# Packed attention before two feed-forward blocks: values loaded in long runs, 32x32 products, exponentials turned by VectorE, no zero-padded scores

## The chip, the cores and the metric

The kernel runs on one core of a Trainium2 chip. A run is one launch of the whole program; its time is the device time in microseconds (us). Before the change three runs gave 1664.1, 1665.73 and 1666.33 us, median 1665.73.

## What is computed

The inputs are q, k and v of shape (8 batches, 8 heads, 576 rows, 64) and p of shape (8, 8, 32, 64). For each batch and head the 32 packed queries p attend to k and v, and q then attends to the 32 results. The output, 4608 tokens of 512 features, goes through two feed-forward blocks:

```python
def sm_attn(qq, kk, vv):
    s = scale * np.matmul(qq, kk.transpose(0, 1, 3, 2))
    s = s - np.max(s, axis=-1, keepdims=True)
    a = np.exp(s)
    a = a / (np.sum(a, axis=-1, keepdims=True) + 1e-09)
    return np.matmul(a, vv)
p_packed = sm_attn(p, k, v)
out = sm_attn(q, p_packed, p_packed)
...
xn = x / rms * rms_g
g = xn @ w_gate
silu = g * (1.0 / (1.0 + np.exp(-g)))
x = silu * (xn @ w_val) @ w_out
h = x @ w_in
out = (h * np.cos(h)) @ w_out
```

Sums and products are in float32; the weights come as float64 and are narrowed to float32 on the chip.

## The kernel before, in words

The program has three parts. The **key stage** computes p_packed for all batches and heads, the middle part runs the first feed-forward block beside the second attention of the batches 1 to 7, and the last part runs the second block. The change touches the key stage alone.

The key stage is the loop `for i in range(NG + 2)` with NG = 16. A step i works on one group of four heads, whose four times 32 packed queries fill 128 partitions. Its work is spread over three steps of the loop, in an order written out by hand (`tc.manual_schedule()`), so that each engine runs its instructions in the order of the code:

- `load_k(i + 4)` and `load_v(i + 2)` issue the loads of k, p and v on the DMA queue of SyncE (SP). One k tile holds 18 rows of 64 values per partition, one run of 4608 bytes. One v tile is laid out as 4 heads x 6 rows per partition on 96 partitions, shifted by 16 (`V_P`), with zeros around them; it is loaded by three DMAs of 32 partitions each, in runs of 6 rows, 1536 bytes. There are three v tiles (`v_t`), used in turn.
- `u_prep` and `u_kt` turn p (`pt`) and k (`kp`, nine transposes) on TensorE. VectorE copies p back (`pT`), ScalarE copies k back (`kT`).
- `u_s1` computes the scores `s`: eight products, 64 rows of k deep. For i < S_PAD = 11 the stationary operand is padded with zeros from 32 to 128 columns, and the four heads add into the same 128 partitions. For i >= 11 each head writes its own 32 partitions. VectorE takes the maximum.
- `u_e` computes the exponentials `e` on ScalarE, into one buffer with 16 zero columns on either side (`e_pad`).
- `u_et`, one step later, turns e by six TensorE transposes of 96 (padded to 128) columns, which ScalarE copies back (`eT`).
- `u_pp`, in the same step, multiplies by v: 24 products, 128 rows deep, 32 columns out, 64 wide, into `pp`. VectorE then scales `pp` by the reciprocal of the sum into `cd` (two buffers), which SP stores to DRAM as `c`.
- `u_fin`, another step later, turns `cd` (`tp`), stores it as `q` through `tf`, and keeps it for the weights (`ppT`).

Beside this the loop carries two kinds of background work. From i = 1 to 16 it loads 19 pieces of the first block's weights (`w_load`, tile `wo`, 512 KB each) and narrows each in the next step: ScalarE takes the upper half (`w_prep(n, 0)`), VectorE runs four passes over it (`w_prep(n, 1)`, lines 143 to 153, called by `w_late`), and every second result is stored as `wy`. From i = 5 on it also carries the second attention of batch 0, as a generator that is advanced by three steps in each pass (`bg0_step`), with instructions on TensorE (`qtp`, `sp`, `xp`), ScalarE (`sq`) and VectorE (`at`, `ssq`). Three products of packed values and weights (`unit`, tile `mps`) lie in the passes 6, 10 and 14.

The order inside one pass decides what waits:

```python
        if 0 < i <= NG: u_et(i - 1)
        if i < NG: u_s1(i)
        ...
        bg0_step(i, 1)
        if 0 < i <= NG: u_pp(i - 1)
        ...
        bg0_step(i, 0 if i == U_ATT else 2)
        ...
        load_v(i + 2)
```

The stores that a pass collects are issued at the top of the next pass (`store(0)`), after the loads of weights and of k and ahead of `load_v`. PSUM buffers of the tag `kp` (four) are shared by `pt`, `kp`, `et`, `tp` and `pp` in turn.

When the loop has ended, TensorE begins the first block with the products `gv` (line 158), which need the second attention of batch 0 (`apt`). On ScalarE's queue the split of `apt` stands behind the last `tf`.

Of the kernel before, what the change touches and what calls it, by code (L numbers as in the profile page):

```python
# [9 lines left out]
F32 = mybir.dt.float32  # L10
F32R = mybir.dt.float32r
I32 = mybir.dt.int32
AF = mybir.ActivationFunctionType
# [7 lines left out]
def kernel(  # L21
# [14 lines left out]
    nc = tc.nc  # L36
    B, H, S, D = q.shape
    NP = p.shape[2]
# [3 lines left out]
    CP = 96  # L42
    NC_ = S // CP
    HALF = S // 2
    CH = NC_ // 2
# [4 lines left out]
    NG = 2 * B  # L50
# [9 lines left out]
    BG_B, KP_B = 2, 4  # L60
    WO_U = 4
    REST = S - 512
    V_P = 16
    R_LOAD, R_SPLIT, S_AT = (1, 2), (4, 5), (20, 21, 24 + 1, 24 + 2)
    W_FROM, W_TO = 1, 16
    W_ORD = (0, 1, 2, 3, 16, 4, 5, 6, 17, 7, 8, 18, 9, 10, 11, 19, 12, 13, 14)
    W_KV = 16
    ATT_U, U_ATT = 28, 5
    S_PAD = 11
    U_S = {6: 0, 10: 1, 14: 2}  # L70
    U_AT = {3: (0, 3), 8: (0, 4), 14: (0, 5), 16: (1, 0), 18: (1, 1), 20: (1, 2), 22: (1, 3), 26: (1, 4), 30: (1, 5)}
    U_J = (12, 15, 18, 21, 26, 30)
# [1 line left out]
    B0_W = (15, 16, 17, 18, 19, -4, 20, 21, -5, 22, 23, -6, 0, -7, 0, -8, 0, -9, 0, -10, 0, -11)  # L74
    B0_L, B0_LEAD = {15: (0,), 16: (1, 2), 17: (3,)}, 4
    W_LOAD, W_SPLIT = (4, 6, 14, 16), (9, 11, 17, 19)
    W2_I0, W2_POOL = 28, False
    T_END, F3_B, OWN = 2, 3, 16
    LAG, LAG_B = 3, 4
# [12 lines left out]
    ident = const.tile([128, 128], F32, name="ident")  # L92
# [87 lines left out]
    u5 = ust.enter_context(tc.tile_pool(name="u5", bufs=4))  # L180
    u2 = ust.enter_context(tc.tile_pool(name="u2", bufs=2))
    u1 = ust.enter_context(tc.tile_pool(name="u1", bufs=1))
    ps_2 = pst.enter_context(tc.tile_pool(name="ps_2", bufs=KP_B, space=PSUM))
# [5 lines left out]
    pT = u1.tile([128, 4, 160], F32, name="pT")  # L189
# [141 lines left out]
                fs[word[0]](int(word[1]), int(word[2]))  # L331
            yield nxt[:1]

    v_t = [u2.tile([128, 4, NC_, D], F32, tag=f"vn{x}", name="vn", bufs=1) for x in range(3)]
    for x in range(2):
        nc.vector.memset(v_t[x], 0.0)
    e_pad = u2.tile([128, 2 * V_P + S], F32, tag="e", name="e", bufs=1)
    for x in (slice(0, V_P), slice(V_P + S, 2 * V_P + S)):
        nc.vector.memset(e_pad[:, x], 0.0)
    nat_k, nat_v = {}, {}  # L340
    st = {}

# [10 lines left out]
    def load_v(i):  # L353
        if i >= NG:
            return
        b, g = divmod(i, 2)
        vn = nat_v[i] = v_t[i % len(v_t)]
        vs = v[b, 4 * g:4 * g + 4].rearrange("h (p m c) d -> m p h c d", m=CH, c=NC_)
        for m in (0, 2, 1):
            nc.sync.dma_start(out=vn[V_P + m * 32:V_P + (m + 1) * 32], in_=vs[m])  # L360

    load_k(0)
    for i in range(2):
# [7 lines left out]
    def u_prep(i):  # L371
        pn, kn = nat_k.pop(i)
        z = st[i] = {}
        nc.gpsimd.tensor_copy(pn[:, 1], pn[:, 0])
        pt = ps_2.tile([128, 128], F32, tag="kp", name="pt")
        nc.tensor.transpose(pt, pn.rearrange("p a d -> p (a d)"), ident)
        nc.vector.tensor_copy(pT[:, :, :NP], pt.rearrange("p (h n) -> p h n", h=4))
        z["kT"], z["kn"] = u1.tile([128, 4, HALF], F32, tag="kT", name="kT"), kn

    def u_kt(i, ms):  # L380

        z = st[i]
        kT, kn = z["kT"], z["kn"]
        kv = kT.rearrange("q h (t m p) -> q h t m p", t=CH, m=CH)
        for m in ms:
            kp = ps_2.tile([128, CH * 128], F32, tag="kp", name="kp")
            for t in range(CH):
                r = 2 * (CH * m + t)
                nc.tensor.transpose(
                    kp[:, t * 128:(t + 1) * 128], kn[:, r:r + 2, :].rearrange("p c d -> p (c d)"), ident  # L390
                )
            nc.scalar.activation(
                out=kv[:, :, :, m, :], in_=kp.rearrange("q (t h p) -> q h t p", t=CH, h=4), func=AF.Copy
            )

    def u_s1(i):
# [4 lines left out]
        for h in range(4):  # L401
            for r, rows in enumerate((top, bot)):
                if i < S_PAD:
                    nc.tensor.matmul(
# [11 lines left out]
    def u_e(i):  # L416
        z = st[i]
        s1, mx = z["s1"], z["mx"]
        e = e_pad[:, V_P:V_P + S].rearrange("p (a s) -> p a s", a=2)
        nc.scalar.activation(  # L420
            out=e, in_=s1[:, :, :HALF], func=AF.Exp, scale=scale, bias=mx[:, 1:2], accum_out=mx[:, 2:3]
        )

    def u_et(i):
        z = st[i]
        eT = u2.tile([128, NC_, 128], F32, tag="eT", name="eT", bufs=1)
        for hf in range(2):
            et = ps_2.tile([128, CH, 128], F32, tag="kp", name="et")
            for c in range(CH):
                cc = hf * CH + c  # L430
                nc.tensor.transpose(et[:, c, :], e_pad[:, cc * CP:cc * CP + 128], ident)
            nc.scalar.activation(out=eT[:, hf * CH:(hf + 1) * CH], in_=et, func=AF.Copy)
        z["eT"], mx = eT, z["mx"]
        nc.vector.tensor_scalar(out=mx[:, 2:3], in0=mx[:, 2:3], scalar1=1e-9, scalar2=None, op0=ALU.add)
        nc.vector.reciprocal(out=mx[:, 3:4], in_=mx[:, 2:3])

    def u_pp(i):
        b, g = divmod(i, 2)
        z = st[i]
        eT, vn, mx = z["eT"], nat_v.pop(i), z["mx"]  # L440
        pp = ps_2.tile([128, D], F32, tag="kp", name="pp")
        for c in range(NC_):
            for h in range(4):
                r = slice(h * NP, (h + 1) * NP)
                nc.tensor.matmul(
                    pp[r], eT[:, c, r], vn[:, h, c % CH * 2 + c // CH, :], start=c == 0, stop=c == NC_ - 1
                )
        cd = u2.tile([128, 2, D], F32, tag="cd", name="cd", bufs=2)
        nc.vector.tensor_scalar(
            out=cd, in0=pp.unsqueeze(1).to_broadcast([128, 2, D]), scalar1=mx[:, 3:4], scalar2=None, op0=ALU.mult  # L450
        )
        stores.append((c_dram[b][:, g, :], cd[:, 0, :]))
        z["cd"] = cd

    def u_fin(i):
        z = st[i]
        b, g = divmod(i, 2)
        tp = ps_2.tile([128, 4, NP], F32, tag="kp", name="tp")
        nc.tensor.transpose(tp.rearrange("p h n -> p (h n)"), z["cd"].rearrange("p a d -> p (a d)"), ident)
        tf = u2.tile([128, 4, NP], F32, tag="tf", name="tf", bufs=3)  # L460
        nc.scalar.activation(out=tf, in_=tp, func=AF.Copy)
        stores.append((q_dram[b][:, 4 * g:4 * g + 4, :], tf))
        n, t = b % 4, ppT[b // 4]
        nc.vector.tensor_tensor(
            out=t[:, 4 * g:4 * g + 4, n * NP:(n + 1) * NP], in0=tp,
            in1=gT[:, 4 * g:4 * g + 4].unsqueeze(2).to_broadcast([128, 4, NP]), op=ALU.mult
        )
        st.pop(i)
# [4 lines left out]
    def w_load(n):  # L473
        if n >= W_KV:
            wo_load(n - W_KV)
            return
        wy_load(n)
# [57 lines left out]
    def b0_load(x):  # L535
        if x < len(B0_W) and B0_W[x]:
            n = B0_W[x]
            (wy_load if n >= 0 else wo_load)(abs(n))
# [63 lines left out]
    def w_due(i):  # L602
        a, b = (n_w * max(0, min(x, W_TO) - W_FROM) // (W_TO - W_FROM) for x in (i, i + 1))
        return [W_ORD[x] for x in range(a, b)]
# [10 lines left out]
    order.enter_context(tc.manual_schedule())  # L615
    u_prep(0)
    u_kt(0, range(CH))
    nc.gpsimd.memset(v_t[2], 0.0)
    w_q, wo_q = [], []
    w_late = lambda: None  # L620
    for i in range(NG + 2):
        due = list(w_due(i))
        for n in due:
            w_load(n)
        load_k(i + 4)
        for n in B0_L.get(i, ()):
            b0_load(n)
        if i == 1:
            load_q()
            load_q()  # L630
        store(0)
        if i == U_ATT:
            att_load(0)
            att_load_c(0)
        if 0 < i <= NG:
            u_et(i - 1)
        if i < NG:
            u_s1(i)
        if i + 1 < NG:
            u_prep(i + 1)  # L640
            u_kt(i + 1, [0, 1])
        if 1 < i:
            u_fin(i - 2)
        if i <= NG:
            w_late()
        if i < NG:
            u_e(i)
        if i + 1 < NG:
            u_kt(i + 1, [2])
        for n in w_q:  # L650
            w_prep(n, 0)
        for n in wo_q:
            wo_split(n - W_KV, 0)
        bg0_step(i, 1)
        if 0 < i <= NG:
            u_pp(i - 1)
        if i in U_S:
            unit(0, U_S[i])
        bg0_step(i, 0 if i == U_ATT else 2)
        w_last = w_late  # L660

        def w_late(ns=tuple(w_q), os=tuple(wo_q)):
            for n in ns:
                w_prep(n, 1)
            for n in os:
                wo_split(n - W_KV, 1)
        if i < NG:
            w_late()
            w_late = lambda: None
        wo_q = [n for n in w_q if n >= W_KV]  # L670
        w_q = due
        load_v(i + 2)
# [187 lines left out]
    for i in range(len(seq) + LAG):  # L860
        b, f, hf = seq[min(i, len(seq) - 1)]
        j = i - b * B1
        if i < len(seq):
# [11 lines left out]
            t = gv_block(b, hf, f)  # L875
# [137 lines left out]
    for i in range(len(seq) + LAG_B):  # L1013
        if i < len(seq):
            n, f = seq[i]
# [16 lines left out]
        if LAG_B <= i < len(seq) + LAG_B - T_END:  # L1032
            n, f = seq[i - LAG_B]
# [33 lines left out]
```

## Time and profile before

| | us |
|---|---|
| median of three runs (1664.1 to 1666.33) | 1665.73 |
| the profiled execution | 1664.63 |
| its span | 1662.8 |
| its key stage, from the start of the span to the first `gv` product | 155.6 |
| TensorE (PE) busy, whole span | 1607.7 (97%) |
| VectorE (DVE) busy, whole span | 1006.9 (61%) |
| ScalarE (ACT) busy, whole span | 809.6 (49%) |

The span is the profiled time from the first to the last instruction of the core; 1.8 us of the execution's own time lie around it. [...] A TensorE product of float32 operands shows as two records, so 24 products are 48 records.

### The profile page before, as it was taken

How to read it: one execution, taken by the hardware profiler on the slowest of the kernel's cores; microseconds unless marked ns; L12 is line 12 of the kernel's file. 1: busy time of each engine (PE TensorE's matmuls, PEld its weight loads, DVE VectorE, ACT ScalarE, POOL GpSimd, SP SyncE). 2: the span in 40 equal slices, each digit the busy share in tenths (PEclk: the TensorE clock that was granted, in tenths of full speed). 3: DMA queues.
4: the chain of work that ended last, by engine and by line, in shares of the span. 5: the costliest groups of instructions: out<-in, count | busy, mean ns of one | idle time of the engine just before them, and what ended most of it. 6: DMA issues, size and time to landing. Idle time of an engine off the chain costs nothing.

```text
span 1662.8 us, 25654 instructions
## 1 busy us (share of the span) xinstructions
PE 1607.7 (97%) x9920; PEld 1308.2 (79%) x9920; DVE 1006.9 (61%) x1890; ACT 809.6 (49%) x1519; POOL 74.9 (5%) x74
## 2 busy tenths in 40 slices
PE   7767989999999999999999999999999999999998
PEld 5545768787888888888988888888888888888887
DVE  3567985666666656564426665656565656565554
ACT  3455554444454444443425555545454545454443
POOL 1000540000000000000210000000000000000000
PEclk9787999999999999999999999999999999999999
DMA  9996754454645453533372110101010101000001
GB/s 235 266 268 198 227 165 153 155 189 145 198 140 185 147 196 131 169 125 110 112 257 77 38 38 1 51 1 51 1 51 0 51 1 51 1 10 16 1 26 26
DMA packets 103577, 177.31 MB, mean 107 GB/s; under 512 B 39456, under 2 KB 55840, under 8 KB 103456
## 3 DMA queue, kind: packets, MB, share of 16 engines
q1 hardware_dynamic: 103456, 175.68, 34.9%
q8 instruction: 78, 1.28, 0.3%
q14 instruction: 43, 0.35, 0.1%
HBM read 134.22 MB, written 41.42 MB: 106 GB/s over the span
## 4 chain that ended last, share of the span: by engine, by line
PE 89%; DVE 4%; DMA 3%; ACT 1%; issue 1%; POOL 0%; SPq 0%; DVEq 0%; ACTq 0%; POOLq 0%
PE hp L159 8%; PE hp L160 8%; PE hp L158 8%; PE ops L160 8%; PE ops L159 8%; PE ops L158 8%; PE gv L158 6%; PE acc L158 6%; PE gv L159 6%; PE acc L160 6%; PE gv L160 6%; PE acc L159 6%; PE mps L565 3%; DMA c<-cd 2%; PE qtp L229 1%
## 5 line engine op out<-in xcount | busy, mean ns | idle before, releaser
L158 PE MATMUL gv<-apt,wmhl 128*128 128x288 f32 x768 | 234.0, 305 | 2.0 <-ACT apt L106 0.9
L159 PE MATMUL gv<-apt,wmhl 128*128 128x288 f32 x768 | 227.8, 297 | 0.4 <-DVE apt L107 0.4
L160 PE MATMUL gv<-apt,wmhl 128*128 128x288 f32 x768 | 226.8, 295 | 0.0
L159 PE MATMUL hp<-xhl,wmhl 128*128 128x512 f32 x576 | 224.1, 389 | 0.0
L160 PE MATMUL hp<-xhl,wmhl 128*128 128x512 f32 x576 | 224.1, 389 | 0.0
L158 PE MATMUL ops<-w2hl,ghl 128*128 128x512 f32 x576 | 224.1, 389 | 0.0
L159 PE MATMUL ops<-w2hl,ghl 128*128 128x512 f32 x576 | 224.1, 389 | 0.0
L158 PE MATMUL hp<-xhl,wmhl 128*128 128x512 f32 x576 | 223.9, 389 | 0.0
L160 PE MATMUL ops<-w2hl,ghl 128*128 128x512 f32 x576 | 222.3, 389 | 0.0
L966 ACT ACTIVATE r<-r 128x512 f32<-128x512 f32 x144 | 91.0, 632 | 250.0 <-DVE r L965 250.0
L974 DVE TENSOR_TENSOR r<-r,hp 128x512 f32<-128x512 f32 x144 | 98.9, 687 | 164.7 <-ACT r L967 164.7
L758 ACT ACTIVATE shl<-silu 128x288 fp32r<-128x288 f32 x192 | 85.4, 445 | 201.6 <-DVE silu L751 201.6
L158 PEld LDWEIGHTS gv<-apt,wmhl 128*128 128x128 f32 x768 | 145.0, 189 | 49.0 <-issue 15.3
L158 PE MATMUL acc<-shl,wohl 128*128 128x512 f32 x432 | 175.4, 406 | 1.1 <-ACT wohl L528 0.9
L160 PE MATMUL acc<-shl,wohl 128*128 128x512 f32 x432 | 170.4, 394 | 2.8 <-POOL wohl L531 2.8
L159 PE MATMUL acc<-shl,wohl 128*128 128x512 f32 x432 | 169.6, 393 | 0.0
L961 ACT ACTIVATE kk<-hp,magic 128x512 f32<-128x512 f32 x144 | 99.1, 688 | 117.4 <-PE hp L160 117.2
L751 DVE TENSOR_TENSOR silu<-silu,gv 128x288 f32<-128x288 f32 x192 | 86.4, 450 | 106.8 <-PE gv L160 81.9
L159 PEld LDWEIGHTS gv<-apt,wmhl 128*128 128x128 f32 x768 | 145.0, 189 | 5.9 <-DVE apt L107 0.6
L160 PEld LDWEIGHTS gv<-apt,wmhl 128*128 128x128 f32 x768 | 144.9, 189 | 0.0
L962 DVE TENSOR_SCALAR kk<-kk 128x512 f32<-128x512 f32 x144 | 61.4, 426 | 116.2 <-ACT kk L961 116.1
L159 PEld LDWEIGHTS ops<-w2hl,ghl 128*128 128x128 f32 x576 | 108.2, 188 | 22.6
(122 smaller groups left out, 2624.6 us busy)
## 6 DMA issues: line engine op xcount, KB each, us to landing
wy<-wy SPq DMA_DIRECT2D x96, 512.0 KB, 4.6
kn<-in_k_dram SPq DMA_DIRECT2D x16, 576.0 KB, 7.9
vn<-in_v_dram SPq DMA_DIRECT2D x48, 192.0 KB, 6.7
qnat<-in_q_dram SPq DMA_DIRECT2D x32, 288.0 KB, 4.1
x_dram<-x SPq DMA_DIRECT2D x18, 512.0 KB, 3.0
x1raw<-x_dram SPq DMA_DIRECT2D x18, 512.0 KB, 3.9
raw<-in_moe_w_in_dram SPq DMA_DIRECT2D x16, 512.0 KB, 4.3
raw<-in_moe_w_out_dram SPq DMA_DIRECT2D x16, 512.0 KB, 4.3
```

The costliest lines, as they stand in the source:

```text
L158: nc.tensor.matmul(ps, lhi, rhi, start=first, stop=False)
L159: nc.tensor.matmul(ps, lhi, rlo, start=False, stop=False)
L160: nc.tensor.matmul(ps, llo, rhi, start=False, stop=last)
L229: nc.tensor.transpose(tp[:, c * CP:(c + 1) * CP], qv[:, i, 2 * c:2 * c + 2, :].rearrange("p c d -> p (c d)"), ident[:CP, :CP],)
L565: nc.tensor.matmul(ps[kt][h * NP:(h + 1) * NP], ppT[b // 4][rows, 4 * kt + h, n:n + NP], w_y[2 * u + kt][rows, j], start=True, stop=True,)
L751: nc.vector.tensor_tensor(out=t, in0=t, in1=pss[1], op=ALU.mult)
L758: nc.scalar.activation(out=sh[:, 0, cols], in_=t, func=AF.Copy)
L961: nc.scalar.activation(out=kk, in_=hp, func=AF.Identity, scale=1.0 / TWO_PI, bias=magic[:, 0:1])
L962: nc.vector.tensor_scalar(out=kk, in0=kk, scalar1=-MAGIC, scalar2=None, op0=ALU.add)
L966: nc.scalar.activation(out=r, in_=r, func=AF.Abs)
L974: nc.vector.tensor_tensor(out=r, in0=r, in1=hp, op=ALU.mult)
```

## The change

Six edits, all in the key stage:

1. One v tile is now loaded like k, by one DMA on 128 partitions in runs of 18 rows (4608 bytes), into four buffers instead of three; the zero fills are gone.
2. The keys are written to `kT` in the order that fits this layout.
3. The exponentials are turned by VectorE, as 32x32 blocks in one instruction of 576 columns; the six TensorE transposes and the two ScalarE copies of each group are gone.
4. The product with v runs as 72 products of 32 rows and 32 columns instead of 24 of 128 rows.
5. The scaling of `pp` into `cd` is a function of its own (`u_cd`), called behind the narrowing at the end of a pass, and `cd` has four buffers instead of two (`tf` four instead of three). `pT` is copied back by ScalarE instead of VectorE.
6. S_PAD is 0: no scores are padded.

```diff
-    S_PAD = 11
+    S_PAD = 0
...
-    v_t = [u2.tile([128, 4, NC_, D], F32, tag=f"vn{x}", name="vn", bufs=1) for x in range(3)]
-    for x in range(2):
-        nc.vector.memset(v_t[x], 0.0)
-    e_pad = u2.tile([128, 2 * V_P + S], F32, tag="e", name="e", bufs=1)
...
-        vn = nat_v[i] = v_t[i % len(v_t)]
-        vs = v[b, 4 * g:4 * g + 4].rearrange("h (p m c) d -> m p h c d", m=CH, c=NC_)
-        for m in (0, 2, 1):
-            nc.sync.dma_start(out=vn[V_P + m * 32:V_P + (m + 1) * 32], in_=vs[m])
+        vn = nat_v[i] = u5.tile([128, CH * NC_, D], F32, tag="vn", name="vn", bufs=VB)
+        nc.sync.dma_start(out=vn, in_=v[b, 4 * g:4 * g + 4].rearrange("h (p c) d -> (h p) c d", c=CH * NC_))
...
-        nc.vector.tensor_copy(pT[:, :, :NP], pt.rearrange("p (h n) -> p h n", h=4))
+        nc.scalar.activation(out=pT[:, :, :NP], in_=pt.rearrange("p (h n) -> p h n", h=4), func=AF.Copy)
...
-        kv = kT.rearrange("q h (t m p) -> q h t m p", t=CH, m=CH)
+        kv = kT.rearrange("q h (c p) -> q h c p", p=NP)
...
-        e = e_pad[:, V_P:V_P + S].rearrange("p (a s) -> p a s", a=2)
+        e = z["e"] = u2.tile([128, 2, HALF], F32, tag="e", name="e", bufs=1)
...
-        eT = u2.tile([128, NC_, 128], F32, tag="eT", name="eT", bufs=1)
-        for hf in range(2):
-            et = ps_2.tile([128, CH, 128], F32, tag="kp", name="et")
-            for c in range(CH):
-                cc = hf * CH + c
-                nc.tensor.transpose(et[:, c, :], e_pad[:, cc * CP:cc * CP + 128], ident)
-            nc.scalar.activation(out=eT[:, hf * CH:(hf + 1) * CH], in_=et, func=AF.Copy)
+        eT = u2.tile([128, 2, HALF // NP, NP], F32, tag="eT", name="eT", bufs=1)
+        nc.vector.transpose(eT.rearrange("p a c n -> p (a c n)"), z["e"].rearrange("p a s -> p (a s)"))
...
-        for c in range(NC_):
+        n_c = CH * NC_
+        for c in range(n_c):
             for h in range(4):
                 r = slice(h * NP, (h + 1) * NP)
                 nc.tensor.matmul(
-                    pp[r], eT[:, c, r], vn[:, h, c % CH * 2 + c // CH, :], start=c == 0, stop=c == NC_ - 1
+                    pp[r], eT[r, c % 2, c // 2], vn[r, c], start=c == 0, stop=c == n_c - 1
                 )
-        cd = u2.tile([128, 2, D], F32, tag="cd", name="cd", bufs=2)
+        z["pp"] = pp
+
+    def u_cd(i):
+        b, g = divmod(i, 2)
+        z = st[i]
+        pp, mx = z["pp"], z["mx"]
+        cd = u2.tile([128, 2, D], F32, tag="cd", name="cd", bufs=4)
...
         if i < NG:
             w_late()
             w_late = lambda: None
+        if 0 < i <= NG:
+            u_cd(i - 1)
```

What this does to the order of instructions is shown at three places. First TensorE, from the end of the pass that multiplies by the values to the next pass (`pp` is the product with v, `et` the turned exponentials, `s` the scores, `pt` and `kp` the turned p and k). Before:

```order
L389 MATMUL kp<-ident,kn 128x128 x3
L445 MATMUL pp<-vn,eT 32x64 x24
L431 MATMUL et<-ident,e 128x128 x6
L404 MATMUL s_578<-kT,pT 128x288 x8
L376 MATMUL pt<-ident,pn 128x128
```

With the change:

```order
L381 MATMUL kp<-ident,kn 128x128 x3
L432 MATMUL pp<-vn,eT 32x64 x72
L400 MATMUL s_811<-kT,pT 32x288 x8
L368 MATMUL pt<-ident,pn 128x128
L381 MATMUL kp<-ident,kn 128x128 x6
```

The six transposes are gone, the scores are 32 columns wide instead of 128, and there are three times as many products with v.

Second VectorE, one pass with one piece of weights (`mx` is the maximum and the sum, `cd` the scaled result, lines 143 to 153 the narrowing). Before:

```order
L434 TENSOR_SCALAR mx<-mx 128x1
L435 RECIPROCAL mx<-mx 128x1
L412 TENSOR_REDUCE mx<-s_675 128x1
L413 TENSOR_SCALAR mx<-mx 128x1
L377 COPY pT<-pt 128x4x32
L464 TENSOR_TENSOR ppT_175<-tp,gT 128x4x32
L449 TENSOR_SCALAR cd<-pp,mx 128x128
L143 TENSOR_SCALAR wy<-wy 128x512
L145 TENSOR_SCALAR wy<-wy 128x512
L149 SCALAR_TENSOR_TENSOR wy<-wo,wy 128x512
L153 SCALAR_TENSOR_TENSOR wy<-wo,wy 128x512
```

With the change:

```order
L419 STREAM_TRANSPOSE eT<-e 128x576
L421 TENSOR_SCALAR mx<-mx 128x1
L422 RECIPROCAL mx<-mx 128x1
L404 TENSOR_REDUCE mx<-s_675 128x1
L405 TENSOR_SCALAR mx<-mx 128x1
L457 TENSOR_TENSOR ppT_175<-tp,gT 128x4x32
L143 TENSOR_SCALAR wy<-wy 128x512
L145 TENSOR_SCALAR wy<-wy 128x512
L149 SCALAR_TENSOR_TENSOR wy<-wo,wy 128x512
L153 SCALAR_TENSOR_TENSOR wy<-wo,wy 128x512
L442 TENSOR_SCALAR cd<-pp,mx 128x128
```

The transpose stands at the head of the pass, the copy of `pT` has left this engine, and `cd` has moved from ahead of the narrowing to behind it.

Third the DMA queue of SP, the same pass (`q`, `c` and `wy` are stores, the others loads). Before:

```order
L350 DMA kn<-in_k_dram 128x1152
L578 DMA q_72<-tf 128x128
L578 DMA c_65<-cd 128x64
L578 DMA wy_80<-wy 128x1024
L360 DMA vn<-in_v_dram 32x4x384 x3
```

With the change:

```order
L344 DMA kn<-in_k_dram 128x1152
L571 DMA q_72<-tf 128x128
L571 DMA wy_80<-wy 128x1024
L571 DMA c_65<-cd 128x64
L352 DMA vn<-in_v_dram 128x1152
```

The store of `c` now stands behind that of `wy`, and the three loads of v have become one.

## Rows read from the trace of the kernel before

**Rows 1.** Page, the span in 40 slices of 41.6 us.
```profile
PE   7767989999999999999999999999999999999998
...
PEclk9787999999999999999999999999999999999999
DMA  9996754454645453533372110101010101000001
```

**Rows 2.** Key stage: stretch, us, busy PE PEld DVE ACT POOL, clock, DMA share, GB/s.
```profile
0.00:32.50 32.50, 25.39 (x284) 18.81 (x284) 11.55 (x31) 14.18 (x33) 4.35 (x20) 1.00 0.99 235
32.50:115.30 82.80, 59.22 (x746) 39.94 (x744) 49.39 (x122) 39.05 (x93) 2.20 (x9) 0.80 1.03 268
115.30:155.60 40.30, 26.79 (x417) 17.15 (x416) 27.88 (x70) 21.26 (x52) 1.64 (x2) 0.78 0.78 210
```

**Rows 3.** Chain that ended last, 0 to 160 us: start, us, what.
```profile
30.18 9.20 DMA c<-cd
...
95.96 7.29 DMA c<-cd
```

**Rows 4.** Waits, 0 to 160 us: total, times, longest, in us.
```profile
POOL pn L374 <- DMA pn<-in_p_dram: 82.5, 12, 12.4
...
DVE cd L449 <- DMA c<-cd: 21.5, 6, 8.2
```

**Rows 5.** Three short stretches, columns as in Rows 2.
```profile
25.00:30.00 5.00, 5.00 (x81) 3.90 (x81) 3.39 (x9) 2.93 (x9) 0.24 (x1) 1.00 1.09 213
105.00:107.50 2.50, 2.50 (x54) 1.88 (x52) 2.37 (x6) 0.91 (x3) 0.29 (x1) 0.50 1.05 386
97.50:100.00 2.50, 1.81 (x16) 0.18 (x12) 2.42 (x8) 0.66 (x2) 0.00 (x0) 1.00 1.03 334
```

**Rows 6.** DMA packets by size: 25 to 30 us, then 105 to 107.5 us.
```profile
DMA packets 719, 1.06 MB, mean 213 GB/s; under 512 B 64, under 2 KB 700, under 8 KB 719
...
DMA packets 544, 0.96 MB, mean 386 GB/s; under 512 B 236, under 2 KB 349, under 8 KB 544
```

**Rows 7.** Groups by line and form, 0 to 160 us: busy us, mean ns, idle before.
```profile
L432 ACT ACTIVATE eT<-et 128x384 f32<-128x384 f32 x32 | 14.6, 493 | 7.1 <-PE et L431 6.5
...
L377 DVE COPY pT<-pt 128x128 f32<-128x128 f32 x16 | 4.5, 281 | 0.0
...
L276 DVE STREAM_TRANSPOSE at<-s 128x576 f32<-128x576 f32 x2 | 1.5, 766 | 0.0
```

**Rows 8.** TensorE in order of time (start, us): clock 1.00, then 0.50 from 106.13 on.
```profile
25.41 0.88 PE L445 MATMUL pp<-vn,eT 128*32 128x64 f32 x48
...
26.22 0.87 PE L431 MATMUL et<-ident,e 128*128 128x128 f32 x6
27.02 2.21 PE L404 MATMUL s<-kT,pT 64*128 64x288 f32 x16
...
101.03 0.72 PE L408 MATMUL s<-kT,pT 64*32 64x288 f32 x16
...
106.13 1.51 PE L445 MATMUL pp<-vn,eT 128*32 128x64 f32 x48
...
113.86 1.54 PE L431 MATMUL et<-ident,e 128*128 128x128 f32 x6
115.33 1.14 PE L408 MATMUL s<-kT,pT 64*32 64x288 f32 x16
```

**Rows 9.** TensorE in order of time: the scores of four passes, and one `mps`.
```profile
85.69 2.21 PE L404 MATMUL s<-kT,pT 64*128 64x288 f32 x16
...
91.86 2.21 PE L404 MATMUL s<-kT,pT 64*128 64x288 f32 x16
...
126.05 1.21 PE L408 MATMUL s<-kT,pT 64*32 64x288 f32 x16
...
136.29 1.21 PE L408 MATMUL s<-kT,pT 64*32 64x288 f32 x16
...
140.87 1.09 PE L565 MATMUL mps<-wy,ppT 64*32 64x512 f32 x16
```

More of the change, by code (lines that the diff above doesn't have):

```diff
@@ L62 @@
     REST = S - 512
-    V_P = 16
     R_LOAD, R_SPLIT, S_AT = (1, 2), (4, 5), (20, 21, 24 + 1, 24 + 2)
@@ L76 @@
     W_LOAD, W_SPLIT = (4, 6, 14, 16), (9, 11, 17, 19)
+    VB = 4
     W2_I0, W2_POOL = 28, False
@@ L332, in attend @@
             yield nxt[:1]
-    v_t = [u2.tile([128, 4, NC_, D], F32, tag=f"vn{x}", name="vn", bufs=1) for x in range(3)]
-    for x in range(2):
-        nc.vector.memset(v_t[x], 0.0)
-    e_pad = u2.tile([128, 2 * V_P + S], F32, tag="e", name="e", bufs=1)
-    for x in (slice(0, V_P), slice(V_P + S, 2 * V_P + S)):
-        nc.vector.memset(e_pad[:, x], 0.0)
     nat_k, nat_v = {}, {}
@@ L392, in u_kt @@
             nc.scalar.activation(
-                out=kv[:, :, :, m, :], in_=kp.rearrange("q (t h p) -> q h t p", t=CH, h=4), func=AF.Copy
+                out=kv[:, :, CH * m:CH * (m + 1), :], in_=kp.rearrange("q (t h p) -> q h t p", t=CH, h=4), func=AF.Copy
             )
@@ L437, in u_pp @@
     def u_pp(i):
-        b, g = divmod(i, 2)
         z = st[i]
-        eT, vn, mx = z["eT"], nat_v.pop(i), z["mx"]
+        eT, vn = z["eT"], nat_v.pop(i)
         pp = ps_2.tile([128, D], F32, tag="kp", name="pp")
-        for c in range(NC_):
+        n_c = CH * NC_
+        for c in range(n_c):
             for h in range(4):
@@ L459, in u_fin @@
         nc.tensor.transpose(tp.rearrange("p h n -> p (h n)"), z["cd"].rearrange("p a d -> p (a d)"), ident)
-        tf = u2.tile([128, 4, NP], F32, tag="tf", name="tf", bufs=3)
+        tf = u2.tile([128, 4, NP], F32, tag="tf", name="tf", bufs=4)
         nc.scalar.activation(out=tf, in_=tp, func=AF.Copy)
@@ L617 @@
     u_kt(0, range(CH))
-    nc.gpsimd.memset(v_t[2], 0.0)
     w_q, wo_q = [], []
```

## The prediction

> **What bounds the kernel now.** I read the 40 slices first, then the busy times by stretch, the chain of waits, the list of waits, and last short stretches and single instructions in order of time.
>
> The slices [rows 1] show two kernels in one. From the fifth slice on TensorE is at 9 tenths in all slices but two early ones, and its clock is granted in full; nothing in the key stage's code can speed that part. The first four slices are the key stage: TensorE at 6 to 9 tenths, its clock at 7 to 9 tenths, and the DMA engines at 9. The change can gain or lose only there, in the 155.6 us before the first `gv` product, and what it gains there the end of the program keeps, since the rest runs on TensorE.
>
> In the key stage no engine is full [rows 2]: between 32.5 and 115.3 us TensorE is busy 59.2 of 82.8 us, VectorE 49.4, ScalarE 39.1. The DMA share is 0.99 and 1.03 up to 115.3 us, so all 16 engines have packets under way, yet they move only 235 and 268 GB/s. After 115.3 us the share falls to 0.78: there something else sets the pace.
>
> The chain of waits blames the stores of `c`: five pieces, the first 9.20 us and the last 7.29 us long [rows 3]. The wait behind them is VectorE's: `cd` has two buffers, and its writer stood 21.5 us in six waits for an older store to land [rows 4]. But the store is slow because it stands in a full queue, and the loads of p, issued well ahead, make POOL wait 82.5 us in twelve waits [rows 4]. So I read the first 115 us as bound by what the DMA engines deliver, with the wait for `c` as the place where it shows.
>
> What do they spend their time on? From 25 to 30 us the packets are nearly all v's: 700 − 64 = 636 of 719 lie between 512 B and 2 KB, which at v's 1536 bytes is 0.98 of 1.06 MB [rows 6], and the rate is 213 GB/s at a share of 1.09 [rows 5]. From 105 to 107.5 us 544 − 349 = 195 packets above 2 KB, the runs of k (4608 bytes) and of the weights, carry most of 0.96 MB, at 386 GB/s and a share of 1.05; the stretch from 97.5 us moves 334 GB/s [rows 5, 6]. The same engines, as busy, move 1.6 to 1.8 times as much when the runs are long and reach all partitions.
>
> **The change part by part.**
>
> *Loads of v.* 16 groups of 3 × 192 KB = 589,824 bytes. At 213 GB/s one takes 2.77 us of the DMA engines. In k's form I take 360 GB/s, the middle of 334 and 386: 1.64 us. Saved: 1.13 us a group. 14 groups are issued before 115.3 us, where the DMA engines are the bound: **−15.8 us**. Ends: at the 268 GB/s that the stretch has as a whole a group takes 2.20 us, and the gain is 8.0; at 386 it takes 1.53, and the gain is 17.4. If v's short runs also hold up the other transfers, and all that is moved from 32.5 to 115.3 us went at 360 GB/s, that stretch would take 82.8 × 268 / 360 = 61.6 us, 21.2 less. That is about as far as it could go: VectorE has 49.4 us of work there, and two passes that did not wait for a store stand 6.2 us apart [rows 9], against 82.8 / 8 = 10.4 on average.
>
> *The wait for `c`* (21.5 us) goes with four buffers. By itself I cost that at nothing, because the full DMA queue covers it: without it VectorE and TensorE would next wait for p and k, as POOL does now. It is what lets the −15.8 through; with two buffers the writer would still meet the queue. Behind the moved `cd` on VectorE stands the next pass's transpose; who waits for `cd` is `tp`, a whole pass later, and the store. SP holds that store ahead of the load of v, so v is issued later in the pass by up to the narrowing. With four v buffers and two passes of lead I cost that at nothing; the cover is the lead of about 16 us. The queue also drops two DMA issues a group.
>
> *TensorE*, per pass at full clock [rows 8]: the turned exponentials go (−0.87), the scores shrink from 2.21 to 0.72 us in eleven passes (−1.49), and the product with v grows from 48 to 144 records. No row shows products of 32 rows and 32 columns on the diagonal. The nearest is the present `pp`, also four products side by side, 0.88 us for 48 records: three times that is 2.64 (+1.76). Net −0.6 in eleven passes, +0.9 in five. At half clock (1.54, 1.14, 1.51) the last five gain 3.02 − 1.54 = +1.5. TensorE is free for 23.6 of 82.8 us and 13.5 of the last 40.3 [rows 2], and `cd` now comes behind 2.2 us of narrowing, so I cost this at nothing inside the loop. In the last pass nothing follows but `cd`, `tp` and `gv`: **+1.0 us** there, the middle of +0.9 and +1.5 less what the narrowing hides; ends 0 and 1.5.
>
> *ScalarE* loses 32 copies of 493 ns (15.8 us by the mean, 14.6 busy) and takes over 16 of 281 ns [rows 7]: 10 us less, hidden, as it is busy half the time.
>
> *VectorE* takes over a transpose of 128x576; the attention's own takes 766 ns [rows 7]. The copy of `pT` (281 ns) leaves. Net +0.49 us a pass. Up to 115.3 us the DMA engines cover that. In the last stretch VectorE has the most work (27.9 of 40.3 us) [rows 2] and the passes follow each other at 10.2 us [rows 9], VectorE's queue waiting in turn for ScalarE and TensorE: five passes, **+2.4 us**; ends 0 and 5 × 0.77 = 3.9.
>
> *The zero fills and the padding of the first scores* shorten the start by up to 3 us; the first loads cover it: 0, end −3.
>
> Sum: −15.8 + 1.0 + 2.4 = −12.4. The profiled execution took 1664.63 (span 1662.8, 1.8 around it), 1.1 below the median and inside the 2.2 us spread of the runs, so I leave the sum on it: 1664.6 − 12.4 = **1652 us**. The case's own range: best 1664.6 − 21.2 − 3 + 2.4 = 1643; worst 1664.6 − 8.0 + 1.5 + 3.9 = 1662.
>
> **The rivals.** A measurement of this kernel can tell about 0.2%, 3.3 us, from no change.
>
> *No change: the passes are paced by VectorE and ScalarE.* If the in-order chain maximum, exponential, narrowing sets 10.2 us a pass already from i = 5 on, as it does from 126 to 136 us [rows 9], then shorter loads only make room in the queue: 82.8 us for eight passes (10.4 each) stays, and +3.4 of added work meets about as much saved before 32.5 us: 1664. Also here: v's runs gain nothing. For it: the last stretch. Against: passes of 6.2 us with the attention beside them, and VectorE only 60% busy before 115.3 us. Chance 0.14.
>
> [...] The granted clock fell to 0.50 in stretches of this stage, after TensorE had stood waiting, and the mean is 0.80 and 0.78 [rows 2]. [...] Chance 0.11.
>
> *Slower by far: the 32x32 products run one after the other.* A transpose of 128 columns takes 0.145 us at full clock, one product of 64 columns half of that; 144 of them take 10.4 us instead of 2.6. A pass is then 1.6 + 0.72 + 10.4 + 1 = 13.7 us, the stage 16 × 13.7 = 220: 1729 us. Against it stands `mps`, where rows 0 to 63 and 64 to 127 write different partitions of the same PSUM tile: 16 records of 512 columns in 1.09 us [rows 9], 68 ns each, where one alone should need 4 × 0.145 = 0.58 us; eight run at a time. Chance 0.03. [...]
>
> **How the numbers follow.** The main case has 0.72. Range 1642 to 1668: from the main case's best end over the no-change case and its measurement (1664 + 3.3); left out are most of the two slow cases, 0.12, and about 0.05 below. Faster 0.72, within 0.2% 0.14, slower 0.14.
>
> **What would show it.** Right: the first `gv` product near 143 us; packets above 2 KB in place of v's, and well over 300 GB/s while the DMA share is near 1; no `cd` waiting for `c`; `pp` near 2.6 us at full clock and 0.77 us for the transpose; passes near 8 to 9 us up to i = 12. Wrong: `gv` still near 155 us with the DMA share below 0.9 before 100 us (VectorE paces), a clock of 0.5 over most of the stage, or `pp` near 10 us.

## The result and the profile after

The changed kernel takes 1680.47 us (median of four runs, 1679.44 to 1684.31) against 1665.89 for the kernel before: ratio 1.0099, interval 1.0081 to 1.0118. It is slower by some 15 us where 1652 was forecast. The profiled execution took 1679.44 us (span 1677.7). The first `gv` product starts at 171.3 us instead of 155.6; those 15.7 us are the whole loss, the rest of the program takes as long as before (0.8 us less).

The page after (lines as in [rows 1], and the queue that the page calls "instruction"):

```profile
PE   6766999999999999999999999999999999999998
...
PEclk9976999999999999999999999999999999999999
DMA  9774755464545454533372020101010101000001
...
q8 instruction: 89, 1.46, 0.4%
```

The key stage by stretch, columns as in [rows 2], with a fourth stretch up to `gv` (the clock is the one granted to TensorE, 1.00 in full; the DMA share is the mean busy share of the core's 16 DMA engines):

```profile
0.00:32.50 32.50, 19.27 (x397) 13.96 (x398) 9.27 (x23) 10.99 (x26) 3.83 (x20) 0.90 0.97 297
32.50:115.30 82.80, 54.19 (x1609) 39.70 (x1607) 52.86 (x122) 35.98 (x89) 2.56 (x8) 0.89 0.82 259
115.30:155.60 40.30, 29.23 (x596) 19.38 (x589) 22.07 (x51) 14.47 (x36) 1.64 (x2) 0.67 0.47 138
155.60:171.30 15.70, 8.92 (x300) 7.75 (x292) 9.53 (x25) 4.51 (x11) 0.00 (x0) 0.67 0.41 117
```

The loads did become cheap: 297 GB/s instead of 235 in the first stretch [rows 2], and the DMA share falls to 0.82 and then 0.47. But no engine took up the room. TensorE is busy 54 of 82.8 us, less than before, with twice as many records (1609 instead of 746). Up to the first `gv` it is busy 111.6 us, as before (111.4), and idle 59.7 us instead of 44.2: the whole loss is idle time. What it waits for, 0 to 171.3 us (total, times, longest, in us; only TensorE's own waits):

```profile
PE tp L452 <- DVE cd L442: 20.9, 11, 5.7
PE pp L432 <- issue: 18.4, 8, 4.3
PE s L400 <- issue: 5.5, 2, 3.4
```

"issue" means that the engine waited for nothing the profile shows. Such waits sum to 24.1 us here (18.4 + 5.5 and small ones); in the same view of the kernel before, up to its `gv`, there is a single one:

```profile
PE pp L445 <- issue: 1.4, 1, 1.4
```

TensorE in order of time shows where they fall (start, us; idle before in brackets):

```profile
29.55 1.07 PE L432 MATMUL pp<-vn,eT 32*32 32x64 f32 x30 [2.69 <-issue]
30.54 1.21 PE L400 MATMUL s<-kT,pT 64*32 64x288 f32 x16
31.68 0.47 PE L368 MATMUL pt<-ident,pn 128*128 128x128 f32 x1
31.95 1.25 PE L381 MATMUL kp<-ident,kn 128*128 128x128 f32 x6
33.03 0.27 PE L452 MATMUL tp<-ident,cd 128*128 128x128 f32 x1
33.14 0.49 PE L381 MATMUL kp<-ident,kn 128*128 128x128 f32 x3
33.56 1.19 PE L432 MATMUL pp<-vn,eT 32*32 32x64 f32 x69
37.74 1.30 PE L432 MATMUL pp<-vn,eT 32*32 32x64 f32 x75 [2.98 <-issue]
...
45.88 1.41 PE L432 MATMUL pp<-vn,eT 32*32 32x64 f32 x62 [4.34 <-issue]
```

TensorE stops in the middle of `pp`, in front of a product that reads the same two tiles as those ahead of it. From one of these stops to the next are 30 + 16 + 1 + 6 + 1 + 3 + 69 = 126 records, and about as many weight loads (PEld, 1607 for 1609 records from 32.5 to 115.3 us). The DMA page of 15 to 47 us, which holds four such stops, shows four packets on the "instruction" queue:

```profile
q8 instruction: 4, 0.07, 0.8%
```

That is 16 KB each, one for some 250 instructions of TensorE; over the whole program it is 89 packets for 2 x 11360 records and weight loads, and in the kernel before 78 for 2 x 9920. Up to `gv` there are 22 such packets, against 11 in the kernel before (before, then after):

```profile
q8 instruction: 11, 0.18, 0.5%
...
q8 instruction: 22, 0.36, 0.8%
```

The trace has each packet's time. The four of 15 to 47 us end at 20.06, 27.96, 36.25 and 44.40 us, and TensorE goes on at 21.48, 29.55, 37.74 and 45.88, which is 1.4 to 1.6 us later each time. So it is with all eleven unexplained waits of 0.2 us or more up to `gv`, the whole 24.1 us: each ends 1.3 to 1.6 us after such a packet. The one wait of the kernel before does too (1.3 us). So the first theory: **TensorE runs out of instructions.** Rivals: `tp` at the head of TensorE's queue waits for a `cd` that now stands behind the narrowing (the 20.9 us above); or TensorE without the padding loses clock.

### The profile page after: what moved, and what is told of

The parts are those of the page before. It is cut to its first block, busy times and chain, and to the rows that moved or that the text cites. A ratio compares the mean times of both kernels' runs of the same rounds, so it can differ in the third digit from the quotient of the medians.

```text
span 1677.7 us, 28455 instructions
## 1 busy us (share of the span) xinstructions
PE 1607.3 (96%) x11360; PEld 1313.1 (78%) x11360; DVE 1012.0 (60%) x1886; ACT 801.7 (48%) x1503; POOL 74.7 (4%) x73
## 4 chain that ended last, share of the span: by engine, by line
PE 90%; DVE 4%; issue 2%; ACT 1%; DMA 1%; POOL 0%; SPq 0%; DVEq 0%; POOLq 0%; ACTq 0%
PE hp L160 8%; PE hp L158 8%; PE hp L159 8%; PE ops L160 8%; PE ops L158 8%; PE ops L159 8%; PE gv L158 6%; PE acc L158 6%; PE acc L160 6%; PE gv L159 6%; PE acc L159 6%; PE gv L160 6%; PE mps L558 3%; PE pp L432 2%; PE qtp L229 1%
## 5 line engine op out<-in xcount | busy, mean ns | idle before, releaser
L160 PEld LDWEIGHTS hp<-xhl,wmhl 128*128 128x128 f32 x576 | 108.2, 188 | 22.6
```

Source lines behind the costliest of these rows:

```text
L160: nc.tensor.matmul(ps, llo, rhi, start=False, stop=last)
```

## Experiments

**Half the instructions, as many columns.** One product takes two rows of v (128 columns).

```diff
...
-        for c in range(n_c):
+        for c in range(0, n_c, 2):
...
-                    pp[r], eT[r, c % 2, c // 2], vn[r, c], start=c == 0, stop=c == n_c - 1
+                    pp[r], eT[r, c % 2, c // 2], vn[r, c:c + 2].rearrange("p c d -> p (c d)"), start=c == 0, stop=c == n_c - 2
...
```

> The changed kernel with the product with v as 36 products of 128 columns instead of 72 of 64: the same columns stream through TensorE, with half the instructions (it leaves half of the exponentials out of the sum, and half of each result unused). Theory A, TensorE's instructions come too slowly: pp keeps its 2.2 us, the idle time that nothing in the profile explains falls from 31 us of the chain to under 10, the key stage ends near 145 us instead of 171, total 1650 to 1660. Theory B, the scaling behind the narrowing holds TensorE up: the wait of tp for cd stays at 20 us and the total at 1676 to 1682. Theory C, the array's clock is lost without the padding: the same columns and clock, total 1676 to 1682.

Measured: 1660.63 us, ratio to before 0.9968 (0.9954 to 0.9982); `gv` at 148.7. TensorE's waits up to there:

```profile
PE tp L452 <- DVE cd L442: 29.7, 15, 5.7
PE pp L432 <- issue: 1.6, 3, 1.1
...
PE s L400 <- issue: 0.9, 1, 0.9
```

The unexplained waits fall from 24.1 to 2.5 us, 21.6 less, and the stage becomes 22.6 us shorter. The two numbers are not one sum: of the 22.6 us, 12.2 are idle time (47.5 instead of 59.7 us) and 10.4 are busy time (101.2 instead of 111.6 us). The products themselves take 2.17 us a group at full clock, as they did; but in the changed kernel TensorE ran at a lower clock behind some of its stops (0.53 from 29.5 to 33 us, where the scores took 1.21 us; 1.00 behind the stop that ends at 37.74, where they took 0.72), and the clock of the whole stage is 0.86 here instead of 0.82. The wait for `cd` is longer than in the changed kernel, and the kernel is faster all the same.

**The padded scores back (S_PAD = 11).**

> The changed kernel with the zero-padded scores of the first eleven groups back (S_PAD 11). Theory A: as many instructions as before this edit, so the gaps stay and the total is 1678 to 1686. Theory B: no change, 1678 to 1684. Theory C: the clock comes back in the first 115 us, total 1665 to 1672.

Measured: 1686.3 us (1.0123, 1.0092 to 1.0154), `gv` at 175.0. The padding brings no time back (the interval lies over that of the changed kernel) and no clock: 0.88 from 32.5 to 115.3 us, as without it (0.89). The theory of the clock falls. The gaps did not stay as expected: TensorE is busy 16.0 us longer, and the unexplained waits fall to 17.2 us.

**`cd` ahead of the narrowing**, right behind `pp`, as before the change.

> The changed kernel with the scaling of pp into cd back ahead of the narrowing, right behind the product with v. Theory A: the unexplained gaps of TensorE stay near 30 us and cd now waits for pp instead of tp for cd, total 1676 to 1684. Theory B: tp no longer waits for cd (20 us of waits gone), total 1660 to 1668. Theory C: 1678 to 1684.

Measured: 1686.8 us (1.0135, 1.0096 to 1.0175), above all three expectations. The wait of `tp` for `cd` falls from 20.9 to 1.0 us, and the unexplained ones rise from 24.1 to 37.7. But these are of two kinds. Nine, 19.6 us, end 1.2 to 1.6 us after an instruction packet, as before this edit. The other eight, 18.0 us, all end 0.1 us after VectorE's transpose of the exponentials (`eT`), which `pp` reads and which still stands behind the narrowing. TensorE now meets VectorE's narrowing at `pp` instead of at `tp`. So this run doesn't say what the wait for `cd` costs. That it doesn't make the loss is shown by the run before, which had 29.7 us of it and was faster than the kernel before.

**The kernel before, its 24 products done three times.**

```diff
-        for c in range(NC_):
+        for x in range(3 * NC_):
+            c = x % NC_
...
```

> The kernel before with its 24 products with v done three times over (72, the sum is three times too large): the instructions of the change without its loads, its transpose, its order of cd or its unpadded scores. Theory A: unexplained gaps on TensorE of 20 us or more appear in the key stage, total 1682 to 1700. Theories B and C: only the array's time is added, 1.8 us a group beside 37 us of free time, total 1666 to 1674, with under 10 us of unexplained gaps.

Measured: 1689.66 us (1.0147, 1.0116 to 1.0177); `gv` at 178.2, 22.6 us later than in the profile of before. The waits:

```profile
PE pp L446 <- issue: 17.7, 6, 4.0
PE s L404 <- issue: 4.7, 1, 4.7
```

22.4 us in place of 1.4, with 23 instruction packets in place of 11; each of these waits ends 1.0 to 1.5 us after a packet. Nothing else of the change is in this run: no 32x32 product, no long run, no moved `cd`. The number of instructions is enough to bring the waits. What they cost in time this run doesn't show: TensorE is also busy 22.1 us longer (133.5 instead of 111.4), and its idle time as a whole is as before (44.7 and 44.2 us), as its other waits became shorter.

**One bank for `pp`, and the products in six pieces between the transposes of k.** The first run is the control of the second.

> The changed kernel with pp in a PSUM bank of its own and three banks instead of four for the other transposes: the control for the run that spreads pp. If the bank ring is no bound: as the changed kernel, 1678 to 1685. If it is: slower than that by up to 10.

> The control with the 72 products of a group issued in six pieces of 12 between the transposes of k, instead of in one piece: as many instructions, as much work. If the supply of instructions is limited in its rate (16 KB in some 8 us beside a full DMA queue): as the control, within 4 us. If it is a delay after a late request, which the lead covers as long as the next instructions are long ones, and which 144 records of 15 ns run through: the gaps shrink, 8 to 20 us faster than the control.

Measured: control 1684.34 (1.0121, 1.0099 to 1.0143), spread 1713.53 (1.0294, 1.0275 to 1.0314). Neither theory had this: the spread is 29 us slower. Six pieces cost more by themselves, at full clock:

```profile
82.49 0.54 PE L436 MATMUL pp<-vn,eT 32*32 32x64 f32 x24
```

6 x 0.54 = 3.2 us instead of 2.21, some 16 us in 16 passes; and the unexplained waits rise from 27.0 to 48.0 us. Only five of them, 7.9 us, end behind an instruction packet, where all 27.0 of the control do. The ten others, 40.2 us, all end 0.1 us after VectorE has turned the exponentials:

```profile
129.51 0.77 DVE L419 STREAM_TRANSPOSE eT<-e 128x576 f32<-128x576 f32 x1
...
130.38 0.86 PE L436 MATMUL pp<-vn,eT 32*32 32x64 f32 x24 [6.94 <-issue]
```

The first of the six pieces stands at the head of the pass, where VectorE still has the narrowing in front of that transpose. So the run is slower by its new order and its pieces. Whether long instructions between the short ones bridge the gaps it doesn't show: the waits behind a packet shrank from 27.0 to 7.9 us, but TensorE also stood 40.2 us in the other waits.

**v loaded four times in all**, with all instructions left, so that the DMA queue carries less.

> The changed kernel with v loaded for the first four groups alone and those four tiles used again, so the DMA queue carries 7 MB less; the products take wrong values from the fifth group on. All instructions of TensorE stay. If the gaps in front of pp come from a DMA queue so full that the blocks of instructions arrive late: the sum of TensorE's waits that nothing explains falls from 24.1 us to under 12 and gv starts 8 to 20 us earlier, 1660 to 1672. If a block takes its time however full the queue is: gaps and time as in the changed kernel, 1675 to 1684.

Measured: 1673.74 us (1.0071, 1.0055 to 1.0088); `gv` at 164.5. Unexplained waits 18.9 us instead of 24.1, all of them ending 1.3 to 1.6 us after a packet. Between the two expectations: at a DMA share of 0.68 instead of 0.82 (32.5 to 115.3 us) the gaps are 5.2 us shorter in all, and most of them stay.

**Fewer instructions and the whole computation: block-diagonal exponentials**, 18 products of 128 rows and 128 columns.

```diff
-            for h in range(4):
-                r = slice(h * NP, (h + 1) * NP)
-                nc.tensor.matmul(
-                    pp[r], eT[r, c % 2, c // 2], vn[r, c], start=c == 0, stop=c == n_c - 1
-                )
+            nc.tensor.matmul(pp, eb[:, c % 2, c // 2], vn[:, c], start=c == 0, stop=c == n_c - 1)
...
```

> The whole computation, with the turned exponentials laid out block by block on the diagonal of a tile of 128 rows and 18 x 128 columns (zeros elsewhere): 18 products of the full array a group in place of 72 of 32x32, so 72 instead of 288 instructions of TensorE. The blocks are put there by two copies on ScalarE and two on POOL; to make room, v has three tiles and cd three. If TensorE's supply of instructions caused the loss: the gaps in front of pp that nothing explains go, gv starts near 148 us as with the products of 128 columns, 1657 to 1663 us. If what cost time was the wait of tp for cd behind the narrowing, which is still here: 1675 or more. If the copies set the pace (ScalarE gets back about 1 us a pass): 1665 to 1672.

Measured: 1791.25 us (1.0774, 1.0747 to 1.0801). All three expectations were far off. The groups of its page say why:

```profile
L440 PE MATMUL pp<-vn,eb 128*128 128x64 f32 x576 | 127.1, 422 | 25.8 <-ACT eb L432 20.6
L440 PEld LDWEIGHTS pp<-vn,eb 128*128 128x128 f32 x576 | 124.1, 332 | 33.7 <-ACT eb L432 27.9
```

127.1 / 16 = 7.9 us a group (the granted clock is 0.50 from 32.5 to 115.3 us), and the weight loads of 128 columns take as long, 124.1 us of busy PEld; 144 records with 32x32 loads took 2.21 us at full clock. I had counted instructions and not their weight loads. The copies also stand ahead of the next p on POOL, and TensorE waited 49.2 us for that p. Unexplained waits are down to 3.5 us. The run says nothing against the supply of instructions.

**Was it the length of v's runs?** The same kernel with v in runs of 1536 bytes, to all 128 partitions:

```diff
-        nc.sync.dma_start(out=vn, in_=v[b, 4 * g:4 * g + 4].rearrange("h (p c) d -> (h p) c d", c=CH * NC_))
+        vs = v[b, 4 * g:4 * g + 4].rearrange("h (p c) d -> (h p) c d", c=CH * NC_)
+        for m in range(CH):
+            nc.sync.dma_start(out=vn[:, m * NC_:(m + 1) * NC_], in_=vs[:, m * NC_:(m + 1) * NC_])
```

> The block-diagonal run with v loaded by three DMAs of 1536-byte runs, each to all 128 partitions, as long as before the change but not to 32 partitions each. If v's old price was the length of its runs: 8 to 16 us slower than the block-diagonal run. If it was the 32 partitions of each load: within 3 us of it.

Measured: 1796.4 us (1.0785, 1.0760 to 1.0810), as the block-diagonal run, but TensorE sets that time. The first stretch, where the queue is full in both, tells more. From 5 to 20 us, columns as in [rows 2], first the kernel before, then this run:

```profile
5.00:20.00 15.00, 13.05 (x95) 9.73 (x99) 2.54 (x8) 5.41 (x13) 0.95 (x4) 1.00 1.04 259
```

```profile
5.00:20.00 15.00, 10.31 (x66) 7.21 (x66) 2.80 (x7) 7.83 (x18) 1.80 (x4) 1.00 1.03 374
```

259 and 374 GB/s, as busy and with v's runs of the same length; the changed kernel, with its runs of 4608 bytes to 128 partitions, moves 371 in the same 15 us. So it is not the length of the runs. What is left is the partitions that a load reaches, or what goes with them. The next runs take the kernel before, with all its instructions of TensorE, and spread v over 96 partitions: by one DMA, by one for each head (the diff), and by heads from partition 0 on.

```diff
-        vs = v[b, 4 * g:4 * g + 4].rearrange("h (p m c) d -> m p h c d", m=CH, c=NC_)
-        for m in (0, 2, 1):
-            nc.sync.dma_start(out=vn[V_P + m * 32:V_P + (m + 1) * 32], in_=vs[m])
+        vs = v[b, 4 * g:4 * g + 4].rearrange("h (p c) d -> h p c d", c=NC_)
+        for h in range(4):
+            nc.sync.dma_start(out=vn[V_P:V_P + CP, h], in_=vs[h])
...
-        kv = kT.rearrange("q h (t m p) -> q h t m p", t=CH, m=CH)
+        kv = kT.rearrange("q h (t p m) -> q h t m p", t=CH, m=CH)
```

> The kernel before, with v in runs of 1536 bytes as it was, but by one DMA to 96 partitions instead of three to 32 each (the keys are numbered so that a partition holds six neighbours; the copies of kT are written with a stride of 3). All instructions of TensorE stay. If v's old price (112 ns for a packet of 1536 bytes) came from the 32 partitions: packets of 65 to 75 ns, some 250 GB/s or more ahead of 115 us, gv up to 13 us earlier, 1652 to 1660. If it came from the run length: packets of 112 ns and 1664 to 1668. If the strided copies of kT cost: slower.

> The kernel before with v in runs of 1536 bytes, one DMA for each head, to 96 partitions from 16 on, so that a DMA reads one unbroken piece of 144 KB. If the order of the rows in DRAM made v's packets slow (106 ns still, in the run with one DMA for four heads): 65 to 80 ns, gv 5 to 13 us earlier than in the profile of before, 1652 to 1661. If the partitions that are reached made them slow: 100 ns or more, 1661 to 1667.

> The same with the 96 partitions from 0 on, as q has them, whose packets of 1536 bytes took 65 ns by the median. If the offset of 16 partitions matters: packets near 65 to 75 ns where those from 16 on have more, and some us faster than that run. If not: as that run.

| v goes to | GB/s, 5 to 20 us | us | ratio to before |
|---|---|---|---|
| 32 partitions at a time (before) | 259 | | |
| 96 from 16, one DMA | 270 | 1662.09 | 0.9992 (0.9977 to 1.0007) |
| 96 from 16, by heads | 284 | 1661.18 | 0.9986 (0.9975 to 0.9997) |
| 96 from 0, by heads | 309 | 1662.50 | 0.9989 (0.9974 to 1.0004) |
| 128 (the block-diagonal kernel above) | 374 | | |

The rate climbs with the partitions, but 96 (270 to 309 GB/s) are far from 128 (374), and none of these times lies 0.2% below before's. What holds the loads to 96 partitions back stays open.

**Four buffers for `cd` alone, and on top of the loads.**

> The kernel before with four buffers for cd and tf, and nothing else. The prediction costs the 21.5 us of wait for the store of c at nothing, as the full queue covers it: 1663 to 1668. If the five pieces of the chain were the bound themselves: 1645 to 1658.

> The same with four buffers for cd and tf, cd in its old place. If the wait of cd for the older store is only the full queue seen in another place: within 3 us of the run with two buffers. If it holds the passes up once the queue is less full: 3 to 8 us faster than that run.

> The same from partition 0 with four buffers for cd and tf: the version that keeps before's few instructions of TensorE and tries for the quicker loads and no wait for the store of c. If v's packets are quick there: 1648 to 1658, faster than both kernels. If they aren't: 1661 to 1666.

Measured: alone on the kernel before 1663.97 (0.9990, 0.9975 to 1.0006), nothing, as the prediction had costed it. With v by one DMA 1661.97 (0.9991, 0.9972 to 1.0010), also nothing. With v by heads from partition 0: **1658.35 us, 0.9972 (0.9956 to 0.9988)**, faster than both kernels, though by 0.28%. Its stage, `gv` at 146.7 us:

```profile
0.00:32.50 32.50, 24.69 (x275) 18.27 (x278) 11.59 (x30) 15.67 (x32) 4.58 (x21) 1.00 0.98 269
32.50:115.30 82.80, 62.70 (x859) 40.93 (x848) 55.21 (x135) 47.21 (x107) 2.48 (x8) 0.86 0.99 276
```

and four long pieces of its chain of waits, from 8 to 19 us (start, us):

```profile
8.21 4.21 PE s L404 x16
13.57 1.25 ACT kT L392 x2
15.53 0.88 PE et L431 x6
16.41 2.14 PE s L404 x16
```

The scores `s` now have 15.7% of the chain, ahead of ScalarE's `kT`, where the stores of `c` led with 22.7% before; loads are still in it (v 4.0%). So the third part of the change was tried there too, the scores without padding; and, with v by one DMA, beside the slower loads:

> The same and no zero-padded scores. By the records' length TensorE has 1.5 us less in eleven passes: 0 to 5 us faster, if TensorE is off the path. If the emptier TensorE loses its clock: 3 to 10 us slower.

> The version that beat both (v by heads to partitions 0 to 95, four cd), without the zero-padded scores: the third part of the change by itself, where the chain now names TensorE's scores first. If TensorE's 1.5 us a pass are on the path there: 3 to 8 us faster, 1650 to 1655. If TensorE loses its clock by the emptier array, as the padded form of the changed kernel did not show: 1661 or more. If neither: 1656 to 1660.

Measured: 1660.58 (0.9992, 0.9974 to 1.0011) with v by one DMA, and 1657.67 (0.9958, 0.9938 to 0.9978) with v by heads from partition 0, `gv` at 149.7. Their intervals lie over those of the same versions with padding; by itself this part makes no difference that these runs can tell.

## Why the prediction was wrong

**The step that failed** is TensorE's: "the product with v grows from 48 to 144 records ... so I cost this at nothing inside the loop". I looked at the records' time alone. That part was good: TensorE's busy time in the stage is 111.6 us where it was 111.4, with 2.21 us for 144 records at full clock where 2.64 was estimated for products side by side and 10.4 for one after the other. But each record comes with a weight load (2885 and 2885 up to `gv`, 1444 and 1444 before), and 22 instruction packets in the stage instead of 11 go with 24.1 us of unexplained waits where 1.4 had been: +22.7 in place of 0. `gv` was forecast near 143 us and came at 171.3, 28.3 later; with half the instructions it comes at 148.7, so 22.6 us hang on the number of instructions (12.2 of idle time and 10.4 of busy time) and 5.7 are left. No rival named this, and a clock of 0.5 over most of the stage, which the prediction gave 0.11, did not come: from 32.5 to 115.3 us it rose from 0.80 to 0.89, and over the whole stage it is 0.82 instead of 0.84.

**The loads of v** (-15.8): right in kind, too large in the sum. The rates came, the DMA share fell, and `cd` waits for no store of `c`. But with half the instructions the stage is 155.6 - 148.7 = 6.9 us shorter, and with quicker loads in the kernel before 155.6 - 146.7 = 8.9, and the medians of the time are 5.8, 5.7 and 7.6 us below before's (half the instructions; spread v with four `cd`, with padding and without): at the lower end of 8.0 or below it. The medians count for more here, because `gv` is read from one profiled execution: the run with four buffers for `cd` alone has it at 149.5, in an execution of 1658.32 us, below its own median of 1663.97. That the engines pace the passes as soon as the loads don't, which was the no-change rival's argument, is how I read the rest: with half the instructions TensorE waits 29.7 us for VectorE's `cd`. No run removes that wait by itself. I also gave two reasons for the rate, "long and reach all partitions"; the 374 GB/s at 1536 bytes rule out the first, and the second is open in part, with 270 to 309 at 96 partitions.

**The wait for `c`**, costed at nothing by itself: right (0.9990). **`tp` waits for `cd` "a whole pass later"**: wrong as a wait, 20.9 us. What it costs stays open: in the run with `cd` first the wait moved to the exponentials that VectorE turns behind the same narrowing.

**VectorE's transpose**: 0.77 us, as said; what it adds on the path (+2.4) no run separates. **ScalarE**: 65.9 busy us up to `gv` instead of 74.5 [rows 2], off the path. **The scores without padding**: no gain that can be told, as in the sum.

## What to carry to other kernels

Count the instructions of an engine, weight loads among them, and not only their time (here the products with v took 2.21 us a group, and 24.1 us went into waits beside them): when short products are cut shorter, see in the timeline whether the engine stops inside a group with "issue" as the reason, and whether the packets of the instruction queue double, as they did here (11 to 22). A wait under "issue" need not be one for instructions: look at what ended just ahead of its end, an instruction packet or the last writer of what the next product reads. A layout that makes the loads cheap has to be charged for the instructions it needs behind them, and the cheap loads are worth only what the next bound leaves, here 6 to 8 us of 16. When a load is slow, look at where its runs go before their length: to 128 partitions, runs of 1536 and of 4608 bytes came in at the same rate here (374 and 371 GB/s).

## What the runs showed of the hardware that was not expected

The queue that the page calls "instruction" moved packets of 16 KB, one for some 127 records of TensorE with their loads (89 for 11360 in the changed kernel, 78 for 9920 before). TensorE stood up to 4.3 us in a wait that ended behind one (4.7 in the tripled kernel, 5.0 in the control with a bank for `pp`), and went on 1.0 to 1.6 us after the packet's end in each of the waits that are put down to instructions here. The gaps did not go when the data queue was emptier (18.9 of 24.1 us left at a DMA share of 0.68 instead of 0.82). Runs of 1536 bytes came in at 259 GB/s to 32 partitions at a time, at 270 to 309 to 96 and at 374 GB/s to 128, with the DMA engines equally busy (shares of 1.03 to 1.06 from 5 to 20 us).
